# Marks of the largest keys kept for the transposed scores, in a fused top-32 attention and expert kernel

## The chip, the core and the metric

The kernel runs on one core of one Trainium2 chip. The metric is the device time of one execution in microseconds (us). The engines are named as in the profile: PE multiplies matrices into PSUM, DVE, ACT and POOL compute on vectors, SP issues DMAs.

## The reference

Attention over 8 batches of 8 heads with 576 positions of 64 dimensions, in which each query keeps its 32 largest scores; then a layer of 8 experts, each of which takes the 576 tokens that rank highest for it (4608 tokens in all).

```python
scores = scale * np.matmul(q, k.transpose(0, 1, 3, 2))
kth = np.partition(scores, -top_k, axis=-1)[..., -top_k:-top_k + 1]   # top_k = 32
scores = np.where(scores >= kth, scores, -1e9)
scores = scores - np.max(scores, axis=-1, keepdims=True)
attn = np.exp(scores); attn = attn / (np.sum(attn, axis=-1, keepdims=True) + 1e-09)
x = np.matmul(attn, v)                      # as [4608, 512], then:
for idx in np.argsort(-(x @ w_gate).flatten()):   # token, expert; cap = 576
    ...
out[mask] = np.maximum(x[mask] @ w1[e], 0.0) @ w2[e]
```

## The kernel before

The first stage, `attention`, goes through 32 pairs of heads, and each pair in 9 tiles of 128 queries (four of the first head, one that holds the last 64 queries of both, four of the second): 288 tiles. Inputs are scaled by 256 and split into two float16 parts, so that float16 products give nearly float32 scores.

`tile_ops` finds the 32nd largest score of each query. PE computes 128 x 576 scores into a PSUM buffer `s` (L213); there are three such buffers. DVE takes the eight largest of each of six chunks of 96 keys (L216, "chunks"), ranks these 48 candidates in five steps (`rank`, L219 to L223) down to the 24th and writes its negative (`minus`, L224). ACT's Sign (L228) marks the keys above this bound: `w` is 1 as a 16-bit integer for them and 0 for the others, which read as float16 is 2^-24 or zero. It also counts them into `acc`. Two matmuls with a scaled identity, `off` (`move`, L231, of 512 and 64 columns), push the marked scores down to -2^60. DVE writes eight extra columns behind the scores (`fill`, L234), which make up for a count that is too small, and takes the eight largest of the 584 columns that are left (`next8`, L235): the last of them is the 32nd. Two more matmuls with `back` bring the marked scores up to +2^60 (L231). Then ACT's Relu (L238) writes `r`, the distance of each score below the 32nd: zero for every key that is kept. This frees the score buffer, and the scores of the third tile after it can go in.

`soft` computes the scores of the tile once more, transposed (keys on partitions), for the first 512 keys: `masks` (L276) puts -2^60 times `r` into a PSUM bank `pt` (a ring of two), `again` (L281, L282) adds the scores, ACT takes the exponent (L286), and POOL splits it into two float16 parts (L289, L292). `tail` does the same for the last 64 keys of all tiles of a pair: eight products with `r` (L314), the scores (L319), the exponent (L336) and the split (L339, L342); `corner` is the block of the last 64 queries and the last 64 keys (L327, L331). `values` multiplies the weights with v: for each tile three float16 products for each 128 keys (L370), where the last 64 keys of each head are the part called `part==1`, and float32 products for the mixed tile (L377). The sums are inverted on DVE (L351, L390) and applied on ACT (L353). `logits` computes the gates (L409, L426).

The order of all of it is written out ahead by `Plan`. Each operation is put on its engine with `at(t, f, pre, take, free, e, d)`: `t` is a priority (the tile's number times PER, plus an offset from the table `O`), `pre` what it depends on, `d` an assumed duration, `take` and `free` a buffer of a ring. `Plan.run` simulates the engines and takes, of the operations that could begin within a window `WIN` of the earliest, the one with the least `t`. Each engine then runs its list in that order and waits on semaphores. So the order changes whenever an offset does, and an instruction that waits holds up all that is behind it on its engine.

The lines around the change:

```python
p=at(t0+O["nt"],minus,[p],e="V",d=.065)
p=at(t0+O["sg"],sign,[p],e="A",d=0.717)
f_=at(t0+O["j8"],fill,[p],e="V",d=0.12)
p=at(t0+O["wm"],lambda: move(off,0),[p],e="P",d=0.216)
p=at(t0+O["wm"]+.001,lambda: move(off,1),[p,f_],e="P",d=0.029)
p=at(t0+O["y8"],next8,[p],e="V",d=0.685)
p=at(t0+O["wb"],lambda: (move(back,0),move(back,1)),[p],e="P",d=0.245)
p=at(t0+O["rl"],relu,[p],take="r",free=[ts],e="A",d=.624); P["tr"][i]=p
```

The second stage, `moe` (from about 950 us), ranks the tokens, gathers them and runs the experts; the diff does not touch it. `redo` recomputes pairs whose counts did not come out, and is skipped otherwise.

Of the kernel before, what the change touches and what calls it, by code (L numbers as in the profile page):

```python
# [99 lines left out]
def attention(tc, q,k,v,w_gate,x_out,L,flags, pairs):  # L100
# [3 lines left out]
    with ExitStack() as ctx:  # L104
# [26 lines left out]
        for i in range(3):  # L131
# [10 lines left out]
        O=dict(ld=65.275, hk=-218.383, hq=41.201, gk=-55.928, gk2=72.94, gq=-255.506, gq2=-136.656, tk=11.004, tk3=-79.989, tq=-138.618, lv=19.887, hv=-42.968, gv=99.377, gv2=35.601, S=-240.511, c0=243.716, c1=-4.066, c2=204.792, c3=-76.567, c4=39.675, c5=168.597, nt=137.483, wb=-67.048, k0=-76.329, k1=-46.874, k2=-138.772, k3=-31.508, k4=61.123, nb=40.395, sg=-78.315, wm=-35.267, y8=-115.191, j8=102.741, rl=-58.771, m1=-54.53, m2=3.089, q2=98.636, t0=45.855, t1=130.568, t2=-48.586, td=-6.338, ex=-59.244, eh=68.337, el=-19.413, u0=7.205, ud=-52.999, ue=1.649, uh=-18.729, ul=-138.955, x0=-115.648, xe=-305.586, xh=-158.146, xl=82.351, v0=-8.899, v1=47.385, v2=34.835, vd=-2.584, vn=-90.833, vs=75.248, lg=63.38, lgd=12.728, l1=-117.561, l2=-7.177, l3=3.808, hg=149.17)  # L142
# [57 lines left out]
        def tile_ops(P,i):  # L200
# [64 lines left out]
        def soft(P,i):  # L265
# [27 lines left out]
            p=tp=at(t0,masks,[P["rel"][i],P["q2"][i//MG]],take="pt",e="P",d=.225)  # L293
            for c in range(4): p=at(t0+O["t2"]+O["td"]*c,lambda c=c: again(c),[p],e="P",d=.116)
# [11 lines left out]
        def tail(P):  # L306

            n=P["n"]; t0=(n*9+8)*PER; D={}; C={}
            def masks():
                D["pt"]=ps_t.tile([128,512],F32,tag="pt",name="pt4")  # L310
                for c in range(4):
                    for h in range(2):
                        j=c if h==0 else 5+c; m0=512 if h==0 else 0
                        T.matmul(D["pt"][h*64:h*64+64,c*128:c*128+128],P["r"][j][:,m0:m0+64],nid60,start=(c==0),stop=False,skip_group_check=True)  # L314
            def again():
                for (K,Q,m) in (("K2","Q1",128),("K3","Q2",66)):
                    for h in range(2):
                        o=D["pt"][h*64:h*64+64,:]; kr=slice(512+64*h,576+64*h); qc=slice(0,512) if h==0 else slice(640,1152)
                        T.matmul(o,P[K][0:m,kr],P[Q][0:m,qc],start=False,stop=(K=="K3"),skip_group_check=True)  # L319
            def expo(nm,w,D):  # L320
                P["e"+nm]=wk.tile([128,w],F32,tag="E"+nm,name="E"+nm,bufs=2)
                A.activation(P["e"+nm],D["pt"][:,:w],AF.Exp,scale=ESC)
            def corner():
                C["pt"]=ps_t.tile([128,512],F32,tag="pt",name="pt4r")
                for h in range(2):
                    o=C["pt"][h*64:h*64+64,0:64]; m0=512 if h==0 else 0; rows=slice(h*64,h*64+64)
                    T.matmul(o,P["r"][4][:,m0:m0+64],nid60[:,rows],start=True,stop=False,skip_group_check=True)  # L327
                for (K,Q,m) in (("K2","Q1",128),("K3","Q2",66)):
                    for h in range(2):
                        o=C["pt"][h*64:h*64+64,0:64]; kr=slice(512+64*h,576+64*h)  # L330
                        T.matmul(o,P[K][0:m,kr],P[Q][0:m,kr],start=False,stop=(K=="K3"),skip_group_check=True)  # L331
            p=tp=at(t0+O["u0"],masks,[P["rel"][8],P["q2"][8//MG]],take="pt",e="P",d=.25)
            pe=p=at(t0+O["u0"]+.02,again,[p],e="P",d=.476)
            def expo4():
                D["E"]=wk.tile([128,512],F32,tag="F",name="F",bufs=PLANBUFS["F"])
                A.activation(D["E"],D["pt"],AF.Exp,scale=ESC)  # L336
            def hi4():
                D["eh"]=wk.tile([128,512],F16,tag="eh4",name="eh4",bufs=2)
                G.tensor_scalar(D["eh"],D["E"],1.0,0.0,op0=ALU.mult,op1=ALU.add)  # L339
            def lo4():  # L340
                el=wk.tile([128,512],F16,tag="el4",name="el4",bufs=2)
                G.tensor_tensor(el,D["E"],D["eh"],op=ALU.subtract); P["e4"]=(D["eh"],el)  # L342
# [3 lines left out]
            p=at(t0+O["x0"],corner,[pe]+[P["soft"][i] for i in range(9)],take="pt",e="P",d=.15); P["done3"]=tp=p  # L346
            for i in range(9): loom.frees(p,P["tr"][i])
            P["te4r"]=P["e4ready"]=at(t0+O["x0"]+O["xe"],lambda: expo("4r",64,C),[p],free=[tp],take="E4r",e="A",d=.11)
# [5 lines left out]
        def values(P):  # L354

            n=P["n"]; hp=P["hp"]; last=[]
            for g in (0,1,2):
# [4 lines left out]
                def dot(j,part,D=D,g=g,begin=begin):  # L362
# [3 lines left out]
                    if g!=1:  # L366
                        e_=P["e"][j if h==0 else 5+j]; out=av[:,j,:]; js=slice(j*128,j*128+128)
                        if part==0: seq=[(e_[x][:,c*128:c*128+128],v_[:,h*5+c,:]) for c in range(4) for (x,v_) in ((0,vh),(0,vl),(1,vh))]
                        else: seq=[(P["e4"][x][:,js],v_[:,h*5+4,:]) for (x,v_) in ((0,vh),(0,vl),(1,vh))]
                        for m_,(a,b_) in enumerate(seq): T.matmul(out,a,b_,start=(part==0 and m_==0),stop=(part==1 and m_==2))  # L370
                    else:
# [10 lines left out]
                for j in range(1 if g==1 else 4):  # L382
                    need=[P["vready"]]+([P["ev"][4],P["e4ready"]] if g==1 else [P["ev"][j if g==0 else 5+j],P["e4op"]])
                    for part in range(1 if g==1 else 2):
                        p=at(t0+O["vd"]*cnt,lambda j=j,part=part,dot=dot: dot(j,part),[p]+need,take="pt" if j==0 and part==0 else None,e="P",d=1.2 if g==1 else .09 if part else .36); cnt+=1
                        if j==0 and part==0: tp=p
# [81 lines left out]
        for n in range(len(pairs)):  # L468
            prep(n); P=Ps[n]; b=P["b"]
            P.update(st=None,tr={},mx={},rel={},q2={},ev={},teh={},soft={},x=[None,None])  # L470
            first=P["hp"]==0
# [522 lines left out]
```

## Time and profile before

| | us |
|---|---|
| median of 3 runs | 1461.5 (1459.62 to 1462.3) |
| the profiled execution | 1458.2 |
| its span, first to last instruction | 1456.5 |
| busy over the span: PE / DVE / ACT / POOL | 1244.9 / 1202.5 / 919.6 / 870.4 |
| mean granted TensorE clock | 0.962 |

Busy times are sums over the whole span, in which two stages with different limits follow each other; the stretches below keep them apart. An instruction's duration runs from its start to its end, and those of one engine overlap: what one costs its engine is the distance from its start to the next start.

### The profile page before, as it was taken

Reading aid. Unit: us, or ns where it says so; the run is one execution under the profiler, and the core shown is the slowest. Engines: PE = TensorE matmul, PEld = TensorE weight load, DVE = VectorE, ACT = ScalarE, POOL = GpSimd, SP = SyncE. Lnnn points to the kernel's source line nnn. Section 1 sums busy time; section 2 is a strip of 40 time slices with the busy share of each in tenths; the row PEclk is TensorE's granted clock in tenths of the full one; section 3 lists DMA queues with packets and bytes.
Section 4 is the critical chain, followed back from the end, with each engine's and each line's share of the span. In section 5 each row is a group of like instructions: output and inputs, shape, how many; then the busy total and the mean of one; then the engine's idle time right before and its main releaser. Section 6 shows DMA issues by size and latency. Waiting matters only on the chain. (4 is left out here: it accounts for less than half of the span.)

```text
span 1456.5 us, 42268 instructions
## 1 busy us (share of the span) xinstructions
PE 1244.9 (85%) x15275; PEld 853.7 (59%) x15276; DVE 1202.5 (83%) x6016; ACT 919.6 (63%) x1994; POOL 870.4 (60%) x1189
## 2 busy tenths in 40 slices
PE   2889888888988988988898998934999999999997
PEld 1556656666665765665665666723655655655663
DVE  4899999899999999998899999667889878878510
ACT  3788788788888888877888888703334424424421
POOL 4788888788788888878878878602023123113211
PEclk8899999999999999999999999955999999999999
DMA  5344464365355355444544443014336446439400
GB/s 119 74 87 85 84 123 92 51 134 102 62 116 108 74 115 98 78 105 96 94 87 106 85 96 78 10 36 148 124 91 199 145 85 199 147 89 274 115 33 33
DMA packets 317963, 148.51 MB, mean 102 GB/s; under 512 B 283440, under 2 KB 299824, under 8 KB 316720
## 3 DMA queue, kind: packets, MB, share of 16 engines
q1 hardware_dynamic: 311856, 126.84, 39.8%
q0 software_dynamic: 5888, 18.88, 4.4%
q8 instruction: 122, 2.00, 0.6%
q14 instruction: 97, 0.79, 0.2%
HBM read 71.34 MB, written 18.87 MB: 62 GB/s over the span
## 5 line engine op out<-in xcount | busy, mean ns | idle before, releaser
L216 DVE MAX8 cd<-s 128x8 f32<-128x96 f32 x1728 | 376.9, 252 | 32.6 <-PE s L213 30.2
L292 POOL TENSOR_TENSOR elm<-F,ehm 128x512 f16<-128x512 f32 x256 | 295.9, 1157 | 12.6
L238 ACT ACTIVATE r<-s,st 128x576 bf16<-128x576 f32 x288 | 213.1, 740 | 59.6 <-PE s L231 50.9
L228 ACT ACTIVATE w<-s,st 128x576 uint16<-128x576 f32 x288 | 213.3, 741 | 53.2 <-DVE st L224 49.7
L235 DVE MAX8 st<-s 128x8 f32<-128x584 f32 x288 | 220.6, 766 | 15.3 <-PE s L231 12.9
L213 PE MATMUL s<-K,Q 128*128 128x512 f16 (+3 forms) x1280 | 191.9, 290 | 29.4 <-DMA Q<-nq 21.4
L289 POOL TENSOR_SCALAR ehm<-F 128x512 f16<-128x512 f32 x256 | 158.3, 621 | 70.4 <-ACT F L286 67.8
L901 PE MATMUL ph<-xT,w1h 128*128 128x288 f16 x1024 | 195.4, 288 | 3.2 <-DMA xT<-xs 1.5
L282 PE MATMUL pt<-Q,K 66*128 66x128 f16 (+1 forms) x1280 | 178.6, 215 | 21.8 <-DMA Q<-nq 21.7
L231 PE MATMUL s<-w,off 128*128 128x512 f16 x576 | 137.7, 288 | 66.6 <-DVE s L234 51.3
L940 POOL DMA_INDIRECT out_dram<-ob,idx x40 | 55.4, 1384 | 221.4 <-ACT ob L935 154.3
L281 PE MATMUL pt<-Q,K 128*128 128x128 f16 (+1 forms) x1280 | 180.0, 215 | 0.0
L213 PEld LDWEIGHTS <-Q 128*128 128x128 f16 (+1 forms) x1280 | 104.7, 101 | 123.1 <-issue 24.3
L286 ACT ACTIVATE F<-pt 128x512 f32<-128x512 f32 x256 | 152.4, 595 | 34.0 <-PE pt L282 27.5
L861 POOL DMA_INDIRECT xg<-x,idx x40 | 51.9, 1297 | 175.6 <-DVE idx L807 107.7
L901 PE MATMUL ph<-xT,w1l 128*128 128x288 f16 x512 | 147.5, 288 | 0.0
L281 PEld LDWEIGHTS <-K 128*128 128x128 f16 x1280 | 117.2, 99 | 40.4 <-issue 27.7
L231 PE MATMUL s<-w,back 128*128 128x512 f16 x576 | 119.3, 289 | 22.0 <-DVE st L235 18.4
L910 ACT ACTIVATE hh<-ph 128x288 f16<-128x288 f32 x128 | 52.4, 410 | 126.9 <-PE ph L901 122.3
L370 PE MATMUL pv<-vh,ehm 128*128 128x65 f16 x1024 | 121.6, 196 | 0.3
L370 PE MATMUL pv<-vl,ehm 128*128 128x65 f16 x1024 | 121.7, 194 | 0.0
L370 PE MATMUL pv<-vh,elm 128*128 128x65 f16 x1024 | 121.3, 194 | 0.0
(268 smaller groups left out, 3373.9 us busy)
## 6 DMA issues: line engine op xcount, KB each, us to landing
wr<-in_moe_w_dram SPq DMA_DIRECT2D x32, 1024.0 KB, 9.7
kn<-in_k_dram SPq DMA_DIRECT2D x64, 128.0 KB, 2.3
qn<-in_q_dram SPq DMA_DIRECT2D x64, 128.0 KB, 2.3
vt<-in_v_dram SPq DMA_DIRECT2D x64, 128.0 KB, 2.7
x<-xb SPq DMA_DIRECT2D x8, 1024.0 KB, 4.4
Q<-nq SPq DMA_TRANSPOSE x160, 3.3
kn<-in_k_dram SPq DMA_DIRECT2D x64, 16.0 KB, 2.2
qn<-in_q_dram SPq DMA_DIRECT2D x64, 16.0 KB, 2.2
```

Of the source, the lines that this page charges most:

```text
L213: T.matmul(s_ps[rows,a:b_],P[Q][:,qc],P[K][:,h*576+a:h*576+b_],start=(Q=="Q1"),stop=(Q=="Q2"))
L216: V.max(D["cd"][:,c*8:c*8+8],D["s"][:,576*c//NCH:576*(c+1)//NCH])
L228: A.activation(D["w"],D["s"][:,:576],AF.Sign,bias=P["st"][:,i,32:33],scale=(1+2.0**-21),accum_out=acc[:,col])
L231: T.matmul(D["s"][:,a:b_],by,w[:,a:b_],start=False,stop=True,skip_group_check=True)
L235: def next8(): V.max(P["st"][:,i,24:32],D["s"][:,:584])
L238: A.activation(r,D["s"][:,:576],AF.Relu,bias=P["st"][:,i,31:32],scale=-1.0)
L281: T.matmul(o,K2[:,kb:kb+128],Q1[:,qc],start=False,stop=False,skip_group_check=True)
L282: T.matmul(o,K3[0:66,kb:kb+128],Q2[0:66,qc],start=False,stop=(c==3 and h==sub[-1][0]),skip_group_check=True)
L289: G.tensor_scalar(D["eh"],D["E"],1.0,0.0,op0=ALU.mult,op1=ALU.add)
L292: G.tensor_tensor(el,D["E"],D["eh"],op=ALU.subtract); P["e"][i]=(D["eh"],el)
L370: for m_,(a,b_) in enumerate(seq): T.matmul(out,a,b_,start=(part==0 and m_==0),stop=(part==1 and m_==2))
L901: P.matmul(B["ph"][:,:288],a[:,c,fs],xT[:,b+c,cs],start=(i==0),stop=(i==11))
```

## The change

Four things change in `attention`. The matmuls with `back` are dropped: relu follows the next-eight pass directly, and leaves 2^49 in `r` for the marked keys (`off` now pushes by 2^49, where it pushed by 2^60). The marks `w` are kept until the pair's corner, in 14 buffers where there were 4, and wherever `r` goes into transposed scores (`masks`, `tail`, `corner`) a second product adds 2^103 times the mark, which cancels what `r` put there. The second matmul with `off` no longer waits for the fill: both go together, and the fill follows them, ahead of the next-eight pass. The weights of the last 64 keys stay float32 and go into one float32 product in `values`, where they were split on POOL and went into three float16 products. And the offsets, PER, SP and the windows of the planner have new values (`O`, left out here).

```diff
-        nid60=cp.tile([128,128],BF16,name="nid60"); V.tensor_scalar_mul(nid60,identf,-(2.0**60))
-        off=cp.tile([128,128],BF16,name="off"); V.tensor_scalar_mul(off,identf,-(2.0**84))
-        back=cp.tile([128,128],BF16,name="back"); V.tensor_scalar_mul(back,identf,2.0**85)
+        nid60=cp.tile([128,128],BF16,name="nid"); V.tensor_scalar_mul(nid60,identf,-(2.0**54))
+        wid=cp.tile([128,128],BF16,name="wid"); V.tensor_scalar_mul(wid,identf,2.0**127)
+        off=cp.tile([128,128],BF16,name="off"); V.tensor_scalar_mul(off,identf,-(2.0**73))
...
-        PER=3.6791; SP=5.5328; MG=3; WPB=14; EHB=14
-        WIN={'V': 0.009, 'A': 0.159, 'G': 0.0, 'P': 0.097, 'D': 2.593}
+        PER=3.8315; SP=5.0791; MG=3; WPB=14; EHB=14
+        WIN={'V': 0.061, 'A': 0.077, 'G': 0.126, 'P': 0.103, 'D': 1.594}
...
-        PLANBUFS=dict(s=3,pt=2,r=WPB,E=3,F=4,eh=EHB,E4=2,E4r=2,xT=2)
+        PLANBUFS=dict(s=3,pt=2,r=WPB,w=WPB,E=3,F=4,eh=EHB,E4=2,E4r=2,xT=2)
...
-                D["w"]=wk.tile([128,576],U16,tag="w",name="w",bufs=4)
+                D["w"]=wk.tile([128,576],U16,tag="w",name="w",bufs=WPB); P["w"][i]=D["w"].bitcast(F16)
...
-            p=at(t0+O["sg"],sign,[p],e="A",d=0.717)
-            f_=at(t0+O["j8"],fill,[p],e="V",d=0.12)
-            p=at(t0+O["wm"],lambda: move(off,0),[p],e="P",d=0.216)
-            p=at(t0+O["wm"]+.001,lambda: move(off,1),[p,f_],e="P",d=0.029)
+            p=P["tw"][i]=at(t0+O["sg"],sign,[p],take="w",e="A",d=0.717)
+            p=at(t0+O["wm"],lambda: (move(off,0),move(off,1)),[p],e="P",d=0.245)
+            p=at(t0+O["j8"],fill,[p],e="V",d=0.12)
             p=at(t0+O["y8"],next8,[p],e="V",d=0.685)
-            p=at(t0+O["wb"],lambda: (move(back,0),move(back,1)),[p],e="P",d=0.245)
             p=at(t0+O["rl"],relu,[p],take="r",free=[ts],e="A",d=.624); P["tr"][i]=p
...
-                pt=D["pt"]; mt=P["r"][i]; first=True
-                for c in range(4):
-                    for (h,rows,qc,oc) in sub:
-                        m0=c*128+64*h
-                        T.matmul(pt[:,c*128+oc.start:c*128+oc.stop],mt[:,m0:m0+128],nid60[:,oc],start=first,**kw); first=False
+                pt=D["pt"]; first=True
+                for (mt,by) in ((P["r"][i],nid60),(P["w"][i],wid)):
+                    for c in range(4):
+                        for (h,rows,qc,oc) in sub:
+                            m0=c*128+64*h
+                            T.matmul(pt[:,c*128+oc.start:c*128+oc.stop],mt[:,m0:m0+128],by[:,oc],start=first,**kw); first=False
...
-                for c in range(4):
-                    for h in range(2):
-                        j=c if h==0 else 5+c; m0=512 if h==0 else 0
-                        T.matmul(D["pt"][h*64:h*64+64,c*128:c*128+128],P["r"][j][:,m0:m0+64],nid60,start=(c==0),stop=False,skip_group_check=True)
+                for (nm,by) in (("r",nid60),("w",wid)):
+                    for c in range(4):
+                        for h in range(2):
+                            j=c if h==0 else 5+c; m0=512 if h==0 else 0
+                            T.matmul(D["pt"][h*64:h*64+64,c*128:c*128+128],P[nm][j][:,m0:m0+64],by,start=(c==0 and nm=="r"),stop=False,skip_group_check=True)
...
-                    T.matmul(o,P["r"][4][:,m0:m0+64],nid60[:,rows],start=True,stop=False,skip_group_check=True)
+                    for (nm,by) in (("r",nid60),("w",wid)): T.matmul(o,P[nm][4][:,m0:m0+64],by[:,rows],start=(nm=="r"),stop=False,skip_group_check=True)
...
-            p=te=at(t0+O["u0"]+O["ue"],expo4,[p],free=[tp],take="F",e="A",d=.48)
-            p=P["te4"]=at(t0+O["u0"]+O["uh"],hi4,[p],take="E4",e="G",d=.59)
-            P["e4op"]=at(t0+O["u0"]+O["ul"],lo4,[p],free=[te],e="G",d=1.115)
+            P["te4"]=P["e4op"]=at(t0+O["u0"]+O["ue"],lambda: expo("4",512,D),[p],free=[tp],take="E4",e="A",d=.48)
...
-            for i in range(9): loom.frees(p,P["tr"][i])
+            for i in range(9): loom.frees(p,P["tr"][i]); loom.frees(p,P["tw"][i])
...
-                        else: seq=[(P["e4"][x][:,js],v_[:,h*5+4,:]) for (x,v_) in ((0,vh),(0,vl),(1,vh))]
+                        else: seq=[(P["e4"][:,js],vt[:,h*5+4,:])]
```

## Rows read from the trace of the kernel before

**Rows 1.** Windows: stretch, its length, busy us of each engine (x instructions), clock, DMA.
```profile
25.00:945.00 920.00, 799.60 (x11752) 583.01 (x11752) 838.22 (x4834) 752.65 (x1707) 752.68 (x1082) 0.99 0.47 91
```

**Rows 2.** Waits of PE, 100 to 850 us: total us, times, longest.
```profile
PE s L231 <- DVE s L234: 41.3, 80, 1.1
...
PE s L231 <- DVE st L235: 12.6, 47, 0.5
```

**Rows 3.** Timeline of DVE, 470 to 480 us: start, duration, line.
```profile
472.31 0.42 DVE L216 MAX8 cd<-s 128x8 f32<-128x96 f32 x2
472.65 0.20 DVE L223 MAX8 st<-cd 128x8 f32<-128x48 f32 x1
...
475.45 0.76 DVE L235 MAX8 st<-s 128x8 f32<-128x584 f32 x1
476.12 0.19 DVE L219 MAX8 st<-cd 128x8 f32<-128x48 f32 x1
476.23 0.21 DVE L234 TENSOR_SCALAR s<-tab,acc 128x8 f32<-128x8 f32 x1
476.36 0.09 DVE L220 MATCH_VALUE_LOAD cd<-st,cd 128x8 f32 x1
...
476.65 0.21 DVE L221 MAX8 st<-cd 128x8 f32<-128x48 f32 x1
476.90 0.09 DVE L222 MATCH_VALUE_LOAD cd<-st,cd 128x8 f32 x1
```

**Rows 4.** Timelines of DVE, ACT and PE: the first and last of 236 tiles.
```profile
98.91 0.16 DVE L224 SCALAR_TENSOR_TENSOR st<-s,st 128x1 f32<-128x1 f32 x1
...
99.17 0.74 ACT L228 ACTIVATE w<-s,st 128x576 uint16<-128x576 f32 x1 [0.62 <-DVE st L224]
...
100.75 0.78 DVE L235 MAX8 st<-s 128x8 f32<-128x584 f32 x1
...
102.02 0.74 ACT L238 ACTIVATE r<-s,st 128x576 bf16<-128x576 f32 x1
...
102.82 0.65 PE L213 MATMUL s<-K,Q 128*128 128x512 f16 x4 [0.37 <-ACT r L238]
...
845.24 0.14 DVE L224 SCALAR_TENSOR_TENSOR st<-s,st 128x1 f32<-128x1 f32 x1
...
845.47 0.74 ACT L228 ACTIVATE w<-s,st 128x576 uint16<-128x576 f32 x1
...
847.46 0.76 DVE L235 MAX8 st<-s 128x8 f32<-128x584 f32 x1
...
848.74 0.74 ACT L238 ACTIVATE r<-s,st 128x576 bf16<-128x576 f32 x1
...
849.60 0.65 PE L213 MATMUL s<-K,Q 128*128 128x512 f16 x4
```

**Rows 5.** Timelines of PE: 405 us, 474 us, and 846 to 850 us.
```profile
405.13 0.19 PE L370 MATMUL pv<-vh,ehm 128*128 128x65 f16 x1
...
405.50 0.20 PE L370 MATMUL pv<-vh,eh 128*128 128x65 f16 x1
...
473.78 0.83 PE L426 MATMUL lg<-wg,xT 128*128 128x8 f32 x6
474.50 0.38 PE L231 MATMUL s<-w,off 128*128 128x512 f16 x1
...
846.35 0.38 PE L231 MATMUL s<-w,off 128*128 128x512 f16 x1
...
848.67 0.41 PE L231 MATMUL s<-w,off 128*128 128x512 f16 x2
848.91 0.39 PE L276 MATMUL pt<-nid,r 128*128 128x128 bf16 x4
849.13 0.22 PE L281 MATMUL pt<-Q,K 128*128 128x128 f16 x1
```

**Rows 6.** Group by line and shape, 200 to 500 us: busy us, mean ns.
```profile
L342 POOL TENSOR_TENSOR el<-F,eh 128x512 f16<-128x512 f32 x11 | 12.7, 1156 | 0.2
```

More of the change, by code (lines that the diff above doesn't have):

```diff
@@ L136, in attention @@
             t=cp.tile([128,10,65],F16,name=f"vl{i}"); VL.append(t); V.memset(t[:,:,64:65],0.0)
-        PER=3.6791; SP=5.5328; MG=3; WPB=14; EHB=14
-        WIN={'V': 0.009, 'A': 0.159, 'G': 0.0, 'P': 0.097, 'D': 2.593}
+        PER=3.8315; SP=5.0791; MG=3; WPB=14; EHB=14
+        WIN={'V': 0.061, 'A': 0.077, 'G': 0.126, 'P': 0.103, 'D': 1.594}
         HG=1.0
         SPLIT=(0,1,2,3,5,6,7,8)
-        PLANBUFS=dict(s=3,pt=2,r=WPB,E=3,F=4,eh=EHB,E4=2,E4r=2,xT=2)
-        O=dict(ld=65.275, hk=-218.383, hq=41.201, gk=-55.928, gk2=72.94, gq=-255.506, gq2=-136.656, tk=11.004, tk3=-79.989, tq=-138.618, lv=19.887, hv=-42.968, gv=99.377, gv2=35.601, S=-240.511, c0=243.716, c1=-4.066, c2=204.792, c3=-76.567, c4=39.675, c5=168.597, nt=137.483, wb=-67.048, k0=-76.329, k1=-46.874, k2=-138.772, k3=-31.508, k4=61.123, nb=40.395, sg=-78.315, wm=-35.267, y8=-115.191, j8=102.741, rl=-58.771, m1=-54.53, m2=3.089, q2=98.636, t0=45.855, t1=130.568, t2=-48.586, td=-6.338, ex=-59.244, eh=68.337, el=-19.413, u0=7.205, ud=-52.999, ue=1.649, uh=-18.729, ul=-138.955, x0=-115.648, xe=-305.586, xh=-158.146, xl=82.351, v0=-8.899, v1=47.385, v2=34.835, vd=-2.584, vn=-90.833, vs=75.248, lg=63.38, lgd=12.728, l1=-117.561, l2=-7.177, l3=3.808, hg=149.17)
+        PLANBUFS=dict(s=3,pt=2,r=WPB,w=WPB,E=3,F=4,eh=EHB,E4=2,E4r=2,xT=2)
+        O=dict(ld=-4.641, hk=-353.547, hq=27.853, gk=75.809, gk2=76.146, gq=-164.926, gq2=-56.244, tk=-65.76, tk3=-64.993, tq=-129.922, lv=-24.1, hv=14.857, gv=160.306, gv2=-21.452, S=-148.895, c0=317.202, c1=114.132, c2=272.013, c3=20.05, c4=13.529, c5=253.783, nt=65.214, k0=-270.58, k1=-26.191, k2=-195.781, k3=3.544, k4=168.29, nb=199.239, sg=-109.565, wm=-61.886, y8=-211.882, j8=202.77, rl=-60.422, m1=-111.093, m2=27.826, q2=8.862, t0=35.36, t1=35.79, t2=-51.349, td=-49.927, ex=-19.166, eh=131.367, el=-124.462, u0=40.181, ud=79.881, ue=81.984, uh=98.302, ul=-116.757, x0=-34.644, xe=-420.431, xh=-61.277, xl=226.181, v0=-8.997, v1=53.057, v2=7.238, vd=-12.719, vn=-218.578, vs=131.073, lg=68.208, lgd=14.575, l1=-123.951, l2=-33.044, l3=3.192, hg=131.403)
         kbase=lambda h,c: (c*128 if h==0 else 640+c*128)
@@ L292, in lo @@
                 G.tensor_tensor(el,D["E"],D["eh"],op=ALU.subtract); P["e"][i]=(D["eh"],el)
-            p=tp=at(t0,masks,[P["rel"][i],P["q2"][i//MG]],take="pt",e="P",d=.225)
+            p=tp=at(t0,masks,[P["rel"][i],P["q2"][i//MG]],take="pt",e="P",d=.45)
             for c in range(4): p=at(t0+O["t2"]+O["td"]*c,lambda c=c: again(c),[p],e="P",d=.116)
@@ L331, in corner @@
                         T.matmul(o,P[K][0:m,kr],P[Q][0:m,kr],start=False,stop=(K=="K3"),skip_group_check=True)
-            p=tp=at(t0+O["u0"],masks,[P["rel"][8],P["q2"][8//MG]],take="pt",e="P",d=.25)
+            p=tp=at(t0+O["u0"],masks,[P["rel"][8],P["q2"][8//MG]],take="pt",e="P",d=.5)
             pe=p=at(t0+O["u0"]+.02,again,[p],e="P",d=.476)
[L334 to L342, printed above, removed]
-            p=te=at(t0+O["u0"]+O["ue"],expo4,[p],free=[tp],take="F",e="A",d=.48)
-            p=P["te4"]=at(t0+O["u0"]+O["uh"],hi4,[p],take="E4",e="G",d=.59)
-            P["e4op"]=at(t0+O["u0"]+O["ul"],lo4,[p],free=[te],e="G",d=1.115)
-            p=at(t0+O["x0"],corner,[pe]+[P["soft"][i] for i in range(9)],take="pt",e="P",d=.15); P["done3"]=tp=p
-            for i in range(9): loom.frees(p,P["tr"][i])
+            P["te4"]=P["e4op"]=at(t0+O["u0"]+O["ue"],lambda: expo("4",512,D),[p],free=[tp],take="E4",e="A",d=.48)
+            p=at(t0+O["x0"],corner,[pe]+[P["soft"][i] for i in range(9)],take="pt",e="P",d=.2); P["done3"]=tp=p
+            for i in range(9): loom.frees(p,P["tr"][i]); loom.frees(p,P["tw"][i])
             P["te4r"]=P["e4ready"]=at(t0+O["x0"]+O["xe"],lambda: expo("4r",64,C),[p],free=[tp],take="E4r",e="A",d=.11)
@@ L368, in dot @@
                         if part==0: seq=[(e_[x][:,c*128:c*128+128],v_[:,h*5+c,:]) for c in range(4) for (x,v_) in ((0,vh),(0,vl),(1,vh))]
-                        else: seq=[(P["e4"][x][:,js],v_[:,h*5+4,:]) for (x,v_) in ((0,vh),(0,vl),(1,vh))]
-                        for m_,(a,b_) in enumerate(seq): T.matmul(out,a,b_,start=(part==0 and m_==0),stop=(part==1 and m_==2))
+                        else: seq=[(P["e4"][:,js],vt[:,h*5+4,:])]
+                        for m_,(a,b_) in enumerate(seq): T.matmul(out,a,b_,start=(part==0 and m_==0),stop=(part==1))
                     else:
@@ L384, in values @@
                     for part in range(1 if g==1 else 2):
-                        p=at(t0+O["vd"]*cnt,lambda j=j,part=part,dot=dot: dot(j,part),[p]+need,take="pt" if j==0 and part==0 else None,e="P",d=1.2 if g==1 else .09 if part else .36); cnt+=1
+                        p=at(t0+O["vd"]*cnt,lambda j=j,part=part,dot=dot: dot(j,part),[p]+need,take="pt" if j==0 and part==0 else None,e="P",d=1.2 if g==1 else .23 if part else .36); cnt+=1
                         if j==0 and part==0: tp=p
@@ L469, in attention @@
             prep(n); P=Ps[n]; b=P["b"]
-            P.update(st=None,tr={},mx={},rel={},q2={},ev={},teh={},soft={},x=[None,None])
+            P.update(st=None,w={},tw={},tr={},mx={},rel={},q2={},ev={},teh={},soft={},x=[None,None])
             first=P["hp"]==0
```

## The prediction

> **What bounds the kernel now.** I read the windows first [rows 1]. The attention stage, roughly 25 to 945 us, is the only one that the diff touches. In it DVE is busy 91% of the time, PE 87%, ACT and POOL 82% each: four engines nearly full, none of them full. Of the waits [rows 2] the reader is to see PE's: it issues in order, and in 750 us it stood 41.3 us in front of the fill's result and 12.6 us in front of the next-eight result.
>
> Busy is not need, though. In the timeline of DVE [rows 3] an instruction that needs nothing from the one before it starts 0.11 us behind a MAX8 of 48 (476.12 to 476.23) and 0.17 us behind one of 96 (two from 472.31 to 472.65), while one that needs the result just written starts 0.25 us behind it (476.65 to 476.90) and the engine counts as busy meanwhile. Start to start, undisturbed, a tile needs 6 x 0.17 for its chunks, 0.67 for the next-eight pass (475.45 to 476.12), 0.13 for the fill (476.23 to 476.36) and 3 x 0.11 for the ranking passes; the two replacing steps with their loads I estimate at 0.17 each, the negated bound and the sums of the values at 0.12 together, all between these spacings: 2.6 us. A tile takes 3.18 us: 236 next-eight passes from 100.75 to 847.46 [rows 4], 746.7 us over 235. DVE has 18% of it to spare.
>
> What holds it back is the ring of three score buffers in PSUM, and the legs of single tiles show it. In the tile whose next-eight pass starts at 100.75, relu ends at 102.02 + 0.74 = 102.76, and new scores for the freed buffer start at 102.82; in the last of the 236, 848.74 + 0.74 = 849.48 and 849.60 [rows 4]. Over all 236 the median from relu's end to the next scores is 0.09 us, three quarters are under 0.31. A buffer is taken again almost as soon as it is free, so the period is a third of the time that a tile spends with its buffer: 9.53 / 3.
>
> **The change part by part.** *The way back is gone.* Before, the next-eight pass is followed by two matmuls and then by relu. From the pass's end to relu's start: 102.02 - 101.53 = 0.49 us in the first tile, 848.74 - 848.22 = 0.52 in the last [rows 4]; over the 236, 0.49 at least, 0.56 in the median. After, relu waits for DVE directly, as sign does for the negated bound today: 99.17 - 99.07 = 0.10 and 845.47 - 845.38 = 0.09 [rows 4], median 0.09. The leg shrinks by 0.47 us; bounds 0.40 (from the least) and 0.67 (from the two means, 0.81 and 0.14, since PE's order sometimes keeps the matmuls back).
>
> *The fill behind the first pass of matmuls.* From sign's end to the next-eight pass: 0.84 and 1.25 us in the two tiles [rows 4], median 1.11. After, the fill waits for both matmuls. On a free path: 0.14 from sign's end to the matmuls (846.21 to 846.35), 0.41 for the pair (the row at 848.67) [rows 5], 0.04 to the reader (half of what 0.49 leaves beside 0.41), and 0.25 from the fill to what needs it. Sum 0.84: the least of today. One turn in DVE's queue and one in PE's go, but the free path is no shorter. Bounds of the saving 0 and 0.25; I take 0.12.
>
> Together 0.59 us of 9.53, 0.197 per tile, and with 288 tiles 57 us (bounds 0.40 x 96 = 38 and 0.92 x 96 = 88), if nothing takes it back.
>
> *What DVE takes back.* Its instructions stay the same in number, but the next-eight pass now needs what the fill just wrote. Where no other tile's instruction lies between, the fill costs 0.25 instead of 0.13, and 0.12 x 288 = 35 us of DVE; where the order puts a chunk between, nothing. The rows show both kinds of spacing [rows 3]. The Trainium skill, page "VectorE: DVE Perf Modes", section "The DRAIN you can't avoid", has it otherwise: the next operation waits for the emptied pipe whether or not a semaphore asks for it, so that only the count of operations matters; by it this term would be zero and the spacings of 0.11 and 0.25 would not differ, as they do here. I take half, 0.06 per tile. DVE's need is then 2.66 of a period of 2.98, its spare share 11% instead of 18%, and tiles that come sooner wait longer for it. About 2.4 us of the 9.53 are such waiting now: a free path is scores 0.65, chunks 5 x 0.17 + 0.25, ranking about 1.5 with each step waiting for the last, sign 0.09 + 0.74, then 0.84, the pass 0.76, 0.49, relu 0.74 and 0.2 of hops. I take half of the 57 as given back, between nothing (DVE at 2.60 of 2.98 has room) and all of it.
>
> *What PE takes on.* Per pair of heads it loses nine times the two matmuls (848.67 to 848.91, 0.24) and gains nine times four products with the marks (848.91 to 849.13, 0.22), and ten small ones for the last 64 keys and the corner at about 0.03. The eight products with float32 weights replace three of 0.031 each (405.13 to 405.50 is twelve) by one that has two records of 0.12 (six float32 records from 473.78 to 474.50) [rows 5]: 8 x (0.24 - 0.093) = 1.18. Sum +1.30 per pair, 0.14 per tile. It lies in the transposed scores and the values, not on a leg of the ring, though it queues ahead of scores. Against it stand 41.3 + 12.6 us in which PE stood still behind fill and next-eight [rows 2], 0.23 per tile, most of which go. I take zero; bounds 41 us lost (0.14 x 288) and 25 won.
>
> *What hides.* POOL loses two operations per pair, the longer of 1.16 us [rows 6], about 0.2 per tile. It is off the ring and at 82%: nothing; were POOL the limit, this would be worth those 0.2. ACT's exponent of the last 64 keys stays. The marks now stay in 14 buffers, like relu's output, and come free with it at the corner; they are taken one leg earlier, some 2.8 us (99.17 to 102.02) of the five tiles, 16 us, by which 14 exceed 9. I cost that at nothing; were the corner late, sign would wait, with relu and the exponents of other tiles behind it on ACT. The diff adds no DMA.
>
> *The new order.* Every priority is new. The trace can't price it: zero, with 15 us (0.05 per tile, a tenth of what DVE has to spare) to either side.
>
> Sum: 57 - 28 = 29 us. The profiled execution took 1458.2 us, so 1429; the median of the runs is 3.3 us above it, which makes 1433.
>
> **Rivals.** *The ring's gain arrives whole* (chance 0.20): DVE has the room and the order fills the gap behind the fill. 57 us, 1404, in 1390 to 1416. For it: the 0.09 us between relu and scores, and PE's 54 us. Against: DVE at 91%. The rule of the Trainium skill that is weighed above would push this way.
>
> *DVE is the bound already* (0.12 for within 0.2%, 0.05 for a gain of 3 to 12 us): what the legs lose, tiles wait in front of DVE. 1461.5. For it: 91% busy. Against: 2.6 us of need in 3.18.
>
> *Slower: the fill exposed* (0.18). DVE can start neither the next-eight pass nor anything queued behind it until the fill has landed, and the fill itself now stands in DVE's order waiting for two matmuls, with other tiles' chunks behind it. Price: 0.12 per tile, 35 us, with the ring's gain nil: 1496; with half of that price, 1479. It decides from the point at which more than 0.2 us per tile is added in front of the next-eight pass, since that eats the 0.197.
>
> The forecast has 0.45, its own range 1416 to 1450. So faster by over 0.2% (3 us, about what a measurement of this kernel tells from none) 0.70, within 0.12, slower 0.18. The range runs from 1398, inside the first rival, to 1466, just inside the slower one.
>
> **What would show it.** In the trace after: next-eight end to relu start near 0.1 us in most tiles; no wait of PE on the fill; next-eight passes about 3.08 us apart; scores still starting about 0.1 us behind relu. Wrong would be: the fill high in DVE's list of waits (slower), the next-eight pass right behind the fill at 0.25 in nearly every tile, scores no longer right behind relu (another bound), or pairs stretched where the float32 products run (PE).

## The result, and the profile after

| | before | after |
|---|---|---|
| median of 19 runs each, us | 1459.62 (1454.53 to 1462.33) | 1472.65 (1464.79 to 1482.35) |
| the profiled execution / its span, us | 1458.2 / 1456.5 | 1472.65 / 1471.0 |
| mean granted TensorE clock | 0.962 | 0.952 |

The changed kernel is slower: ratio 1.0101, interval 1.0086 to 1.0116. Forecast were 1433 us and a chance of 0.70 for faster; the time lies above the range of 1398 to 1466. All of the loss is in the attention stage: its last next-eight pass starts at 948.66 us, before at 934.76, and from there to the end nothing has changed (522 us of span each). Lines shift by one: sign is L229, fill L235, next-eight L236, relu L239, scores L214.

Windows of after: the stretch of [rows 1], the middle of the stage, and two short stretches to which I come below (busy us of PE, PEld, DVE, ACT and POOL, then clock, DMA share, GB/s).
```profile
25.00:945.00 920.00, 821.63 (x12289) 655.12 (x12288) 835.09 (x4838) 740.58 (x1689) 692.68 (x1005) 0.97 0.45 90
100.00:850.00 750.00, 675.20 (x10216) 541.20 (x10214) 681.40 (x3956) 610.18 (x1398) 576.62 (x835) 0.97 0.47 93
306.00:313.00 7.00, 5.45 (x57) 4.62 (x56) 1.04 (x5) 3.00 (x7) 5.10 (x7) 0.90 0.71 226
312.00:317.00 5.00, 5.00 (x31) 3.30 (x31) 3.20 (x23) 0.00 (x0) 0.00 (x0) 0.50 0.27 71
```
Against [rows 1] PE is busier by 22 us, POOL less by 60, and DVE's 838 is 835 in the same 920 us: DVE is not busier, it has come less far.

Waits of after, 100 to 850 us.
```profile
POOL ehm L289 <- ACT F L286: 103.5, 64, 6.7
...
ACT F L286 <- PE pt L282: 37.2, 27, 6.6
...
PE s L232 <- ACT w L229: 24.6, 36, 2.5
PE s L214 <- ACT r L239: 21.1, 56, 1.4
...
DVE cd L217 <- PE s L214: 17.4, 19, 2.6
DVE s L235 <- PE s L232: 16.0, 17, 2.0
...
DVE L L422 <- PE lg L421: 4.3, 4, 2.9
...
DVE L L418 <- PE lg L411: 3.9, 4, 2.8
```
PE's 41.3 us in front of the fill [rows 2] are gone, as forecast; relu follows the next-eight pass by 0.09 us in the median and scores follow relu by 0.06, as forecast too. The passes are 3.20 us apart and not 3.08. New are long single waits: ACT stands 6.6 us before transposed scores, and DVE 2.9 and 2.8 us before gates (L418, L422), where it waited 0.3 us at most before. These name a place; an average over 750 us would not. The next-eight passes show the same: from the first of one pair to the first of the next it mostly takes 26 to 30 us, but 38.9 from tile 81 to 90. Every fourth such gap, ahead of pairs 6, 10, 14 and so on, has a mean of 31.9 us, where it was 28.4 before; five of the seven (38.9, 32.5, 30.4, 33.4, 31.8) make all of the difference.

Timeline of DVE in the longest of them, right before the first tile of pair 10.
```profile
303.35 0.21 DVE L235 TENSOR_SCALAR s<-tab,acc 128x8 f32<-128x8 f32 x1
303.46 0.15 DVE L225 SCALAR_TENSOR_TENSOR st<-s,st 128x1 f32<-128x1 f32 x1
303.59 0.78 DVE L236 MAX8 st<-s 128x8 f32<-128x584 f32 x1
...
305.42 0.23 DVE L235 TENSOR_SCALAR s<-tab,acc 128x8 f32<-128x8 f32 x1 [0.99 <-PE s L232]
305.69 0.78 DVE L236 MAX8 st<-s 128x8 f32<-128x584 f32 x1
...
309.48 0.17 DVE L418 COPY L<-lg 64x8 f32<-64x8 f32 x1 [2.76 <-PE lg L411]
312.53 0.19 DVE L422 TENSOR_TENSOR L<-lg,L 128x32 f32<-128x32 f32 x1 [2.88 <-PE lg L421]
313.06 0.17 DVE L423 TENSOR_TENSOR L<-lg,L 64x8 f32<-64x8 f32 x1 [0.34 <-PE lg L411]
314.13 1.25 DVE L217 MAX8 cd<-s 128x8 f32<-128x96 f32 x7 [0.90 <-PE s L214]
```
And of ACT and PE in the same stretch.
```profile
302.65 0.74 ACT L239 ACTIVATE r<-s,st 128x576 bf16<-128x576 f32 x1
...
304.47 0.77 ACT L239 ACTIVATE r<-s,st 128x576 bf16<-128x576 f32 x1
...
306.55 0.74 ACT L239 ACTIVATE r<-s,st 128x576 bf16<-128x576 f32 x1 [0.83 <-DVE rs L341]
...
309.70 0.66 PE L399 MATMUL ptl<-identf,xb 128*128 128x128 f32 x4 [0.26 <-DVE L L418]
...
311.10 1.39 PE L421 MATMUL lg<-wg,xT 128*128 128x8 f32 x8 [0.64 <-ACT xT L401]
312.42 0.60 PE L411 MATMUL lg<-wgr,xT 128*64 128x8 f32 x4
312.95 3.06 PE L214 MATMUL s<-K,Q 128*128 128x512 f16 x12
```
Relu of the last three tiles frees their buffers at 302.65 + 0.74 = 303.39, at 305.24 and at 306.55 + 0.74 = 307.29. With nothing else in the way scores would follow each 0.1 us later. They come at 312.95, right behind the last product of the gates, and three buffers are filled in a row: the ring had run empty. In 306 to 313 DVE is busy 1.04 us of 7. What it waits for are the gates of pair 7, a chain through PE, ACT and DVE in turn.

Why scores stand behind gates is in the code. The statistics `st` of a pair lie in one of three buffers, so `begin` of pair n depends on `done` of pair n - 3; the loads of v depend on it too (`p3`), and the next pair's loads of q and k on these. For the last pair of a batch `done` is set to the end of the gates, though v is read for the last time by the values and `st` by `clear` (L304), both of which the pair's own `done` already covers. `Plan` does not put a pair's scores into PE's list ahead of what the pair depends on. Before, the gates ended some 18 us ahead of the first scores of the pair that they hold (their last piece on DVE, then the scores of pair 10):

```profile
289.43 0.17 DVE L433 TENSOR_TENSOR L<-lg,L 64x8 f32<-64x8 f32 x1
```
```profile
307.84 0.65 PE L213 MATMUL s<-K,Q 128*128 128x512 f16 x4
```
In after the scores of six of the seven held pairs start right behind the gates' last product; ahead of pair 14, whose gap is 29.5 us, the gates end 8 us earlier. What tells the five pairs with the long gaps apart is how long the first score buffer had then stood free, from the end of relu to the scores that take it: 9.6, 5.8, 5.6, 6.1 and 5.6 us ahead of pairs 10, 18, 22, 26 and 30, 32.5 us in all, and 0.1 us ahead of pairs 6 and 14. The new offsets move the gates to the edge.

### The profile page after: what moved, and what is told of

Read it like the earlier page. It is cut to its first block, busy times and chain, and to the rows that moved or that the text cites. A ratio compares the mean times of both kernels' runs of the same rounds, so it can differ in the third digit from the quotient of the medians.

```text
span 1471.0 us, 43991 instructions
## 1 busy us (share of the span) xinstructions
PE 1279.1 (87%) x16043; PEld 939.2 (64%) x16044; DVE 1200.4 (82%) x6016; ACT 915.7 (62%) x1994; POOL 828.1 (56%) x1125
## 5 line engine op out<-in xcount | busy, mean ns | idle before, releaser
L217 DVE MAX8 cd<-s 128x8 f32<-128x96 f32 x1728 | 362.9, 250 | 41.1 <-PE s L214 39.8
L214 PE MATMUL s<-K,Q 128*128 128x512 f16 (+3 forms) x1280 | 200.9, 301 | 61.5 <-ACT r L239 28.9
L229 ACT ACTIVATE w<-s,st 128x576 uint16<-128x576 f32 x288 | 213.5, 741 | 58.3 <-DVE st L225 51.3
L239 ACT ACTIVATE r<-s,st 128x576 bf16<-128x576 f32 x288 | 214.3, 744 | 45.0 <-DVE st L236 33.6
L236 DVE MAX8 st<-s 128x8 f32<-128x584 f32 x288 | 221.8, 770 | 1.0 <-DVE s L235 0.2
L214 PEld LDWEIGHTS <-Q 128*128 128x128 f16 (+1 forms) x1280 | 110.6, 105 | 163.6 <-issue 58.8
L930 POOL DMA_INDIRECT out_dram<-ob,idx x40 | 64.5, 1614 | 220.0 <-ACT ob L925 143.9
L286 ACT ACTIVATE F<-pt 128x512 f32<-128x512 f32 x256 | 149.3, 598 | 53.2 <-PE pt L282 48.1
L282 PE MATMUL pt<-Q,K 66*128 66x128 f16 (+1 forms) x1280 | 175.1, 218 | 3.6 <-DMA Q<-nq 3.5
L281 PE MATMUL pt<-Q,K 128*128 128x128 f16 (+1 forms) x1280 | 175.3, 218 | 0.0
L232 PE MATMUL s<-w,off 128*128 128x512 f16 x576 | 120.2, 290 | 37.8 <-ACT w L229 36.3
L360 PEld LDWEIGHTS <-ehm 128*128 128x128 f16 x2048 | 118.6, 103 | 11.4 <-issue 5.2
L276 PE MATMUL pt<-nid,r 128*128 128x128 bf16 (+1 forms) x1280 | 116.0, 219 | 6.1 <-ACT F L286 2.9
```

The costliest lines, as they stand in the source:

```text
L214: T.matmul(s_ps[rows,a:b_],P[Q][:,qc],P[K][:,h*576+a:h*576+b_],start=(Q=="Q1"),stop=(Q=="Q2"))
L217: V.max(D["cd"][:,c*8:c*8+8],D["s"][:,576*c//NCH:576*(c+1)//NCH])
L236: def next8(): V.max(P["st"][:,i,24:32],D["s"][:,:584])
L239: A.activation(r,D["s"][:,:576],AF.Relu,bias=P["st"][:,i,31:32],scale=-1.0)
L281: T.matmul(o,K2[:,kb:kb+128],Q1[:,qc],start=False,stop=False,skip_group_check=True)
L282: T.matmul(o,K3[0:66,kb:kb+128],Q2[0:66,qc],start=False,stop=(c==3 and h==sub[-1][0]),skip_group_check=True)
```

## The experiments

Each median stands beside that of the kernel before on the same chip, with the ratio and its interval.

**The old order: marks alone, and all parts.** The first undoes the new order, the fill's place and the float32 weights, and keeps the marks without the way back; the second keeps all parts and has the offsets of before.

```diff
-            p=at(t0+O["wb"],lambda: (move(back,0),move(back,1)),[p],e="P",d=0.245)
+            p=at(t0+O["wb"],lambda: None,[p],e="P",d=0.245)
...
+                for (mt,by) in ((P["r"][i],nid60),(P["w"][i],wid)):
```


> The order of before, instruction for instruction, with one part of the change alone: the matmuls with back are gone, the marks stay in 14 buffers and enter the transposed scores. Fill, float16 split of the last 64 keys and every priority are those of before. If the order is what made the change slow and the ring's gain is real (theory A), this is faster than before by 25 to 45 us, about 1425. If the parts themselves cost it, the added marks on PE or a DVE that is full already (theory B), it is within 5 us of before, or slower. The leg from the next-eight pass to relu should be near 0.1 us under both; only the period tells them apart.

> All parts of the change, in the order of before: marks, fill right ahead of the next-eight pass and behind both matmuls, one float32 product for the last 64 keys. Theory A: faster than before by 10 to 35 us, about 1437, as forecast for the change. Theory B: as slow as the change, 1470 or above, since the parts are all there. What lies between this and the run with the marks alone is the price of fill and float32 together: up to 35 us by the fill exposed, up to 34 us by the float32 products if PE passes on all of it.

Measured: 1464.54 beside 1455.64, ratio 1.0058 (1.0039 to 1.0078); and 1498.35, ratio 1.0278 (1.025 to 1.0306). In the order of before the shorter leg gains nothing, and both runs came out as their theory B had it. They do not tell the order from the parts, the marks' products on PE among them; the runs without the hold do. Timelines of DVE and ACT, marks alone:
```profile
476.36 0.78 DVE L235 MAX8 st<-s 128x8 f32<-128x584 f32 x1
...
476.44 0.94 ACT L355 ACTIVATE xb<-pv,rs 128x64 f32<-128x64 f32 x4
477.22 0.79 ACT L238 ACTIVATE r<-s,st 128x576 bf16<-128x576 f32 x1
```
Relu could start at 477.14 and follows the four scalings in ACT's list. Here its place costs only 0.08 us, but over all tiles the leg from next-eight to relu is 0.53 us in the median, though its least is 0.03: this order still leaves the room that the two matmuls took. The waits say where the rest went:
```profile
PE s L231 <- DVE s L234: 71.1, 124, 1.3
DVE cd L216 <- PE s L213: 24.7, 56, 2.3
```
PE's wait on the fill is 71.1 us where it was 41.3 [rows 2].

**The hold on the gates taken away.** After, with the pair's own values as `done`; the order is worked out anew from the same offsets.

```diff
-                P["done"]=at(P["done"]["t"]+.001,lambda: None,[P["done"],Ps[n-1]["fin"]])
-                logits(P,1); P["done"]=P["fin"]; ...
+                vd=P["done"]; P["done"]=at(P["done"]["t"]+.001,lambda: None,[P["done"],Ps[n-1]["fin"]])
+                logits(P,1); P["lgd"]=P["fin"]; P["done"]=vd; ...
```


> The changed kernel, in which a pair of heads no longer waits to begin until the gates (logits) of the pair three before it are done; it waits for that pair's own values alone, which is all that its buffer needs. The profile after shows pairs of 30 to 39 us at tiles 81, 153, 189, 225, 261, in front of the pairs that wait for gates, beside pairs of 26 to 27. Theory A (stalls of the new order by that wait): no pair above 30 us, and 10 to 20 us less than the change, 1453 to 1463. Theory B (PE or DVE overloaded, the wait only where it shows): the time is lost elsewhere and the result stays within 5 us of 1472.

Measured: 1434.76 beside 1455.64, ratio 0.9847 (0.9816 to 0.9877), 38 us under after (37 by the two ratios), where 10 to 20 were expected. Its windows, its waits of DVE, and DVE around the gates of pair 7:
```profile
100.00:850.00 750.00, 686.53 (x10691) 558.21 (x10689) 713.54 (x4136) 636.67 (x1464) 598.03 (x868) 0.99 0.50 99
```
```profile
DVE s L235 <- PE s L232: 8.3, 17, 1.8
...
DVE cd L217 <- PE s L214: 2.9, 9, 0.7
```
```profile
279.98 0.17 DVE L422 TENSOR_TENSOR L<-lg,L 128x32 f32<-128x32 f32 x1
280.10 0.09 DVE L223 MATCH_VALUE_LOAD cd<-st,cd 128x8 f32 x1
...
280.29 0.22 DVE L235 TENSOR_SCALAR s<-tab,acc 128x8 f32<-128x8 f32 x1
280.42 0.20 DVE L224 MAX8 st<-cd 128x8 f32<-128x48 f32 x1
280.54 0.77 DVE L236 MAX8 st<-s 128x8 f32<-128x584 f32 x1
...
291.02 0.17 DVE L423 TENSOR_TENSOR L<-lg,L 64x8 f32<-64x8 f32 x1
```
The gates now run between tiles: DVE goes on 0.12 us behind the piece that stood alone before, and its wait on scores falls from 17.4 to 2.9 us. Where the time went can be counted. From the first to the last pair after takes 895.2 us and this kernel 855.5. Of the 39.7 us between them the seven gaps ahead of the held pairs hold 32.5 (31.85 and 27.20 us in the mean), the gaps behind these 17 (29.06 and 26.61), and the other 17 gaps give 10 back. In this kernel the first score buffer stands free for 0.2 to 0.5 us ahead of all seven pairs.

The scores do not pass the gates in this run: the gates' last piece starts on DVE at 291.02 and the first scores of pair 10 at 299.17, and ahead of each of the seven pairs the gates end 7.4 to 8.0 us before the scores. Lifting the condition gave an order in which the gates come in time. Whether the statistics or the loads of v were the part of it that counted, this run does not tell.

**Four buffers for the statistics.** If only `st` tied the pair to the gates, one more buffer would move the hold a pair later.

```diff
-                P["st"]=wk.tile([128,9,33],F32,tag="st",name="st",bufs=3)
+                P["st"]=wk.tile([128,9,33],F32,tag="st",name="st",bufs=4)
...
-            pre=[Ps[n-3]["done"]] if n>2 else []
+            pre=[Ps[n-4]["done"]] if n>3 else []
```


> The changed kernel with four buffers for a pair's statistics where there are three: a pair begins when the one four before it is done. The hold on the gates is thereby put off by one pair and not taken away, and the order is worked out anew with it, as it was where the hold was dropped. If the hold is the cost (theory A), the stall moves by a pair (to the tiles around 90 to 99 in place of 81 to 90) and the time stays within 8 us of the change, 1465 to 1480. If the gain of 38 us without the hold was a lucky new order (rival), this may fall as far, 1435 to 1455, or rise, and no pair stands out.

Measured: 1459.18 beside 1456.49, ratio 1.0021 (1.0007 to 1.0035); 12 to 13 us under after, more than I had expected. The long gap did move by one pair (39.4 us from tile 90 to 99, then 32.8 and 36.9), but what ends it is something else. SP's timeline, then the first DVE instruction behind the gap:
```profile
303.48 9.88 SPq L262 DMA_TRANSPOSE Q<-nq  x2
313.41 0.59 SPq L164 DMA_DIRECT2D vt<-in_v_dram  x1
...
318.79 0.79 SPq L159 DMA_DIRECT2D kn<-in_k_dram  x1
...
340.40 1.31 SPq L182 DMA_TRANSPOSE Q<-nq  x1
```
```profile
344.38 1.25 DVE L217 MAX8 cd<-s 128x8 f32<-128x96 f32 x7 [8.35 <-PE s L214]
```
The gates of pair 7 had ended at 316.7. Pair 11 waits for its own q and k: its loads stand in SP's list behind those of v for pair 10, which depend on the same `done` by `p3`, and its last transpose is issued at 340.40. In after the last one had been issued by 298.1, 15 us ahead of the scores. So `done` holds by two routes, `st` and the loads; this run opened the first, and the second closed a pair later.

**The way back returned**, in after's order with the hold, and in that without it. The marks' products go and the three constants of before come back.

```diff
             def relu():
+                move(back,0); move(back,1)
...
-                for (mt,by) in ((P["r"][i],nid60),(P["w"][i],wid)):
+                for (mt,by) in ((P["r"][i],nid60),):
```


> The changed kernel in its new order, with one part undone: the matmuls with back stand again between the next-eight pass and relu, and no marks enter the transposed scores. Theory A: the leg grows by 0.4 us again and the order's stalls stay, so 15 to 40 us slower than the change, 1487 to 1510. Theory B, with the marks on PE as the cost: faster than the change, 1455 to 1468.

> The changed kernel without the hold, its order unchanged, with one part undone: the matmuls with back stand between the next-eight pass and relu again, and no marks enter the transposed scores. It prices the main term of the forecast where nothing stalls on the gates: 0.4 to 0.5 us more on each tile's leg, a third of it in the period, 38 to 57 us less what DVE gave back. Forecast as it stood: 20 to 57 us slower than without the hold, 1455 to 1492, with the period from 3.06 to between 3.13 and 3.26. If the leg is worth nothing by itself (rival: DVE bounds), within 8 us of 1434.8.

Measured: 1525.47 beside 1455.64, ratio 1.0468 (1.0436 to 1.0501), 53 us over after; and 1492.99 beside 1455.05, ratio 1.0258 (1.023 to 1.0286), 58 us over the kernel without the hold. Waits of the second:
```profile
ACT r L240 <- PE s L232: 85.6, 150, 1.5
...
PE s L214 <- ACT r L240: 42.0, 117, 0.8
...
DVE cd L217 <- PE s L214: 30.2, 78, 1.2
```
Relu waits 85.6 us for the two matmuls, scores 42.0 us for relu (16.2 without the way back) and DVE 30.2 us for scores (2.9). That is the ring, link by link, and DVE at its end stands and waits. The price needs care, though. The marks' products leave PE in these runs, and the two matmuls have no place of their own in this order: from the next-eight pass to relu it is 0.91 us in the mean (0.82 in the median), more than the 0.82 (0.56) of before. Against the 0.37 without the hold that is 0.54 us, which at a third of it per tile over 288 tiles makes 52 us of the 58.

**The fill alone, and float32 alone**, each put into the kernel before.

```diff
-            def next8(): V.max(P["st"][:,i,24:32],D["s"][:,:584])
+            def next8(): fill(); V.max(P["st"][:,i,24:32],D["s"][:,:584])
...
-            f_=at(t0+O["j8"],fill,[p],e="V",d=0.12)
+            f_=at(t0+O["j8"],lambda: None,[p],e="V",d=0.12)
```
```diff
-                        else: seq=[(P["e4"][x][:,js],v_[:,h*5+4,:]) for (x,v_) in ((0,vh),(0,vl),(1,vh))]
+                        else: seq=[(P["e4"][:,js],vt[:,h*5+4,:])]
```


> The kernel before with one edit: the fill stands right ahead of the next-eight pass and behind both matmuls with off; back, marks, split and order as before. The fill should cost DVE 0.26 us in place of 0.13 (next-eight start 0.25 behind the fill's), so 0.13 x 288 = 37 us if DVE is the bound, and PE loses its wait on the fill (41 us between 100 and 850). I expect slower by 15 to 37 us, 1471 to 1493; a rival in which the way by DVE to PE and back was the cost says faster, by up to 15.

> The kernel before with one edit: one float32 product for the last 64 keys in place of the split on POOL and three float16 products; order as before. PE takes 1.18 us more per pair, 38 us in all, POOL 1.8 us less. If PE passes on what it takes (theory B), 20 to 38 us slower, 1476 to 1494; if it hides (theory A), within 6 us of before. With the run of the fill this adds up to the 34 us between marks alone and all parts in the old order, or it does not.

Measured: 1477.39 beside 1456.49, ratio 1.0135 (1.0113 to 1.0157), 20.9 us; and 1467.88, ratio 1.0083 (1.0067 to 1.0098), 11.4 us. Together 32, about the 34 between the two kernels of the first experiment. In the first of them PE no longer waits for the fill and waits 27.5 us for the marks instead. DVE waits for these matmuls as it did before: 15.7 us ahead of the fill, where it was 12.6 ahead of the fill and 10.9 ahead of the next-eight pass.
```profile
PE s L231 <- ACT w L228: 27.5, 58, 0.8
PE s L231 <- DVE st L235: 27.4, 61, 0.9
...
DVE s L234 <- PE s L231: 15.7, 44, 2.3
```

**The last 64 keys in the kernel without the hold**: the float16 split back on POOL, and, the other way, float16 weights with one float16 product. The second leaves the low parts of these weights and values out.

```diff
-                        else: seq=[(P["e4"][:,js],vt[:,h*5+4,:])]
+                        else: seq=[(P["e4"][:,js],vh[:,h*5+4,:])]
```


> The changed kernel without the hold, and with the weights of the last 64 keys split on POOL again and in three float16 products, everything else and the order as in the run without the hold. It prices the float32 products where nothing stalls on the gates. My term was +1.18 us of PE per pair and -1.8 us of POOL, taken together as nothing. If PE is near its limit (theory B), this is 15 to 35 us faster than without the hold, about 1410; if PE has room (theory A), within 6 us of 1435, or slower by up to 15, since POOL then carries the split at a place where the order left no room for it.

> The changed kernel without the hold, its order unchanged, in which the weights of the last 64 keys are written by ACT as float16 and go into one float16 product; their low parts are left out. It takes the float32 products off PE (0.24 us each, eight per pair, for 0.03: 1.7 us per pair, 54 us in all) and puts no split back on POOL. Theory A (PE has room where nothing stalls): within 8 us of 1434.8. Theory B (PE passes on what the products take): faster by 25 to 54 us, 1381 to 1410.

Measured: 1494.08 beside 1456.49, ratio 1.0259 (1.0236 to 1.0282); and 1426.99 beside 1458.16, ratio 0.9786 (0.9754 to 0.9817). The first missed by far: the split has no place of its own in this order, and PE stands behind it.
```profile
DVE cd L217 <- PE s L214: 43.1, 43, 3.4
...
PE pv L367 <- POOL el L341: 25.0, 25, 1.0
```
It says nothing on float32. The second does: with the float32 product of the last 64 keys gone altogether, the time falls by 8 to 9 us only (7.8 by the medians, 8.9 by the two ratios).

**Other offsets for the same parts**, with the hold and without it; only PER, SP, the windows and `O` differ from after.

```diff
-        PER=3.8315; SP=5.0791
+        PER=4.2646; SP=2.7137
```


> The changed kernel with nothing but other priorities, PER, SP and windows, searched for the parts as they are now; the hold on the gates is left in. If the new order was the loss and the parts pay once the order fits them (theory A), no pair stands out and the result is faster than before by 25 to 45 us, 1412 to 1432. If the hold as such costs, whatever the order (a stronger form of A), the stalls stay and it lies at 1455 or above. If PE or DVE are overloaded by the parts (theory B), it cannot be much below before, 1450 or above.

> The changed kernel without the hold, with priorities searched for it. Theory A: like the run without the hold in the order of the change (1434.8), or faster by up to 20 us. It also tells whether a good order needs the hold dropped: if this and the searched order with the hold lie within 8 us of each other, it does not.

Measured: 1442.68 beside 1458.16, ratio 0.9901 (0.9866 to 0.9935), some 11 us over what I had expected; and 1420.18, ratio 0.9738 (0.9706 to 0.977), the fastest of all, 38 us under before. In the first the gaps ahead of the held pairs are 28.6 us in the mean, those of the others 27.5, and the score buffer stands free for 0.1 us ahead of them: an order can keep the gates early enough and need not stall on the hold. It is slower than the second by 22 us all the same, more than the 8 us within which, by what was expected, the hold would not have mattered, and these gaps do not explain it: in the second they are 28.9 us, and the others 26.9. What else the two orders differ by is open.

## Why the prediction was wrong

**The step that failed** is the last one: "The new order. Every priority is new. The trace can't price it: zero, with 15 us (0.05 per tile, a tenth of what DVE has to spare) to either side." In place of zero it cost some 38 us, and the two edited lines of the run without the hold take that back. The bound was drawn from DVE's spare time per tile. What the order did was no cost per tile but an empty ring ahead of five pairs, and the trace of before could have shown the margin: 18 us between the gates and the first scores of the pair that depends on them. A second step failed as well, the fill, whose sign was wrong.

**The rest of the sum came out nearly, but not by all of its terms.** Forecast were -29 us without that step; the kernel without the hold is 20.9 under before.

*The way back*: taken 0.47 x 96 = 45 us, of a leg of 0.56 that was to become 0.09. The leg is 0.09 in the median in after, and 0.15 without the hold; in the mean it went from 0.82 to 0.29 and 0.37. Without the hold that is 0.45 us less, 43 us at a third of it per tile: the mechanism was right, and so was the size. The 58 us of the run with the way back are the price of a longer leg than that of before.

*The fill*: the sign was wrong. From sign's end to the next-eight pass the mean is 1.47 us in after and 1.44 without the hold, where it was 1.21, and the median went from 1.10 to 1.32; I had taken 0.12 less. The sum for the free path (0.84) was near the least that is seen (0.92), but most tiles lie far above it. In the mean, before and after: from sign to the first matmul 0.50 and 0.47 us, so PE's queue ahead of it stayed; the two matmuls 0.60 and 0.41, so 0.19 was won since the second waits for nothing; from the matmuls' end to the next-eight pass 0.10 and 0.58. The fill used to run meanwhile and now comes behind: 0.31 us until it starts, where the free path had 0.04, and 0.27 from it to the pass. 0.23 to 0.26 us on the ring make 22 to 25 us. Alone, in the old order, the edit cost 20.9, but the leg grew by only 0.18 there and DVE paid the longer spacing of the next paragraph in every tile: that run is no second measurement of the same price.

*DVE's part of the fill*: the order does put an instruction between. In 218 of 234 tiles of after another tile's instruction lies between fill and next-eight pass (303.35, 303.46, 303.59 above; 305.42 and 305.69 is one of the 16 without), so 16 x 0.12 = 2 us and not half of the 35. Where none ever lies between, in the run with the fill alone, the spacing is 0.25 in the median. Among the operations on 8 and 48 columns one that needs the result just written starts 0.23 to 0.27 us behind it, an independent one 0.11 to 0.13. The Trainium skill, page "VectorE: DVE Perf Modes", section "The DRAIN you can't avoid", says that leaving out semaphores does not let the next operation start before the pipe is empty; these spacings do not agree with that. The same section adds that an operation that is not held starts earlier, which the prediction left out, and with that the short spacings agree.

*What DVE takes back*: I let it take 28 of 57 us. In the stage without the hold DVE is busy 713.54 of 750 us, 95%, and there a leg longer by 0.54 us, 52 us by the ring's third, cost 58: nothing was given back. Busy was not need, as the first part says; I then used the busy share as a reason after all.

*PE*: taken as zero. The float32 product is worth 8 to 9 us without the hold and 11.4 in the old order, the direction of the bound of 41 but far less. The four products with the marks take 0.22 us per tile in the median, as forecast; no run took them alone.

So -43, +22 to +25 and +8 to +11 make -7 to -13, and with -58 for the way back -22 to -28; the -20.9 measured lies between. Prices taken in different orders do not add more closely than that. That the forecast of -29 came near is luck: the halving for DVE had stood in for the fill.

**The rivals.** *The fill exposed* was the slower one, and the kernel is slower, but not by it: its sign is there, the fill high among DVE's waits (16.0 us), but its leg is as long in the kernel without the hold, which is faster than before. *DVE is the bound already* falls by the 58 us. *The gain arrives whole* holds for the way back alone, as far as the runs price it.

**What stays open.** The order is worked out anew in each of these kernels, so 38 us is the hold together with the order that follows from lifting it. The count by gaps puts 32.5 of the 39.7 us at the held pairs and 17 right behind them, against 10 the other way that have no such cause. Part of it may be PE's clock: its mean in 100 to 850 us is 0.97 in after and 0.99 without the hold, and no run parts the two. The two kernels with other offsets still differ by 22 us, which the gaps ahead of these pairs do not explain. And with the way back returned the kernel without the hold is 38 us over before; the fill and float32 explain some 30, the leg that is longer than before some more, and what is left may be offsets that suit a kernel without the way back.

## What to carry to other kernels

Where each engine runs a list fixed ahead, an edit that shortens a leg is one thing and the order another: look for every release that a later stage's first instruction depends on, how long before it that release now comes, and price the new order by what happens when that margin is gone. An edit that is put into an order without a place of its own, as the way back and the split here, prices its place along with itself. A buffer should be released by its last reader and not by the end of a longer chain that happens to follow it. Count time per group of tiles before blaming a cost per tile: a loss that sits in one group of four points at what happens once in four, whatever the averages say.

## What the runs showed of the hardware

The granted clock fell right where the ring was to be filled again. In 306 to 313 us PE was busy 5.45 of 7 us and the clock 0.90; in 312 to 317 PE was busy throughout and the clock 0.50, the lower of the two levels (1.2 GHz). The twelve records of scores took 3.06 us there. It fell at three of the other four long gaps too (a mean of 0.66 in 539 to 544 us, 0.50 in 770 to 775, 0.66 in 888 to 893), and not ahead of pair 22 (1.00 in 654 to 659). In the run with four buffers the scores behind the longer gap took 1.64 us, at a clock of 1.00 in 343 to 346:
```profile
343.68 1.64 PE L214 MATMUL s<-K,Q 128*128 128x512 f16 x12
```
There PE had been busy less, 5.03 of the 8 us before. What makes the difference these runs do not settle; where the clock falls, the stall is paid for again in the refill.

A float32 weight load of 128 x 128 took 191 ns, one in float16 for the scores 101.
```profile
L214 PEld LDWEIGHTS <-Q 128*128 128x128 f16 x324 | 30.1, 101 | 38.4 <-issue 15.6 <-DMA Q<-nq 1.3
L360 PEld LDWEIGHTS pv<-vt,E 128*128 128x128 f32 x176 | 26.6, 191 | 0.8
```
